# K and V loaded in tiles of two heads, 4 MB each, in a decode kernel of attention and MLP

## The chip, the core and the metric

The kernel runs on one core of a Trainium2 chip. A core has five engines with queues of their own: PE (matmul), DVE (vector), ACT (scalar functions), POOL and SP. SP here issues nearly all loads. Sixteen DMA engines move data from the chip's memory (HBM) into the core's own (SBUF, 128 partitions). The metric is device time in microseconds (us) of one execution.

## What is computed

One decode step for a batch of B = 4 rows of width D = 576. One branch is attention of 32 query heads over 16 cached key/value heads, of which the last W = 2048 keys count. The other is a small MLP. The input and both branches are summed.

```
xn = layernorm(x)
W  = min(4096, max(256, Sk // 4))                  # Sk = 8192, so W = 2048
q  = (xn @ wq) as [B, 32, 1, 128]
k, v = last W keys of k_cache, v_cache [B, 16, 8192, 128], each head used by rep = 2 query heads
o  = softmax(q k^T / sqrt(128)) v
A  = o as [B, 1, 4096] @ wo
# MLP branch with one token: the shifted parts are zero, so x1 = xn
Bm = xn + gelu(layernorm(xn) @ w3) @ w4
out = x + A + Bm
```

K and V are 33.5 MB each, the four weight matrices 20 MB together.

## The kernel before

**Tiles.** `load_kv` (L103) loads one KV head of all four batch rows as a tile of 2 MB: 32 partitions to a batch row, NC = 64 consecutive keys to a partition, 16 KB in one run. K and V tiles share a pool of six buffers (`NKV`). A DMA splits over the 16 DMA engines, eight partitions to each, so an engine moves eight packets of 16 KB for a tile.

**Loads.** All loads but x stand in SP's queue, in program order. The list `order` is K0 K1 K2 V0 K3 V1 K4 and so on, V13 V14 V15 last. `flush_loads` issues as many as there are free buffers, and the loop frees a K buffer and a V buffer at the end of each head. Ahead of V0, V4, V8 and V12 stands one of the four pieces of wo (L125, 1.18 MB, two buffers, the first of which also holds small early tiles). w3 (L130, L131) stands behind V2 and takes the buffer of wq. The rows of w4 that the tiling leaves over are x4. They lie in a K/V buffer and come in eight small pieces (L164 "A", L167 "B", L170 "C", five at L174), two behind V13, three behind V14, three behind V15 (`X_AFTER`). w4 (L153) comes last, in six pieces, and takes w3's buffer.

**One head.** DVE turns K, two quarters of a tile at a time (`k_transpose`, L256). It works on 32-bit words, each a pair of neighbouring values of the head dimension, so the even and the odd values stand alternately in `kt`, and a score matmul reads every second bf16. `k_mask` (L357) writes a large negative number into the score tile S where key rows and query rows are of different batch rows. `k_scores` adds the products, 16 matmuls of 512 columns a head (L369). Softmax: DVE takes the row maximum (L375, L377), PE brings it to eight rows (L382), DVE reduces and negates it (L387), PE subtracts it from S by a matmul over all 512 columns (L391), ACT takes the exponential with the row sum (L398), and DVE turns it into PT (L403). `pv` multiplies with V, 16 matmuls of 512 columns on four groups of 32 PE columns (L426). ACT scales the result by one over the sum (L433), PE turns it (`o_turn`, four 128x128 blocks in float32, L439), and DVE sums it (L449). For every fourth head `o_spread`, `o_pick` and `o_proj` (L458, L468, L471, L215) multiply by a piece of wo and add to an accumulator of two PSUM tiles, `accs`.

**Order.** The program writes out the order of all engines' work. In round t of the loop head t is scored, head t - 1 goes through softmax, head t - 2 through `pv`, t - 3 and t - 4 through the output. The MLP's first half (`mlp_g`, `mlp_turn`, `mlp_act`) stands in round 7. Behind the loop the last heads are finished, then come x4 and w4 (`mlp_extra`, `mlp_out`, L215), and two copies and a store end the program (L684, L686, L687).

Of the kernel before, what the change touches and what calls it, by code (L numbers as in the profile page):

```python
# [16 lines left out]
NKV = 6  # L17
BIG = 1.0e30
# [4 lines left out]
def kernel(  # L23
# [27 lines left out]
    PB = P // B  # L51
    NC = W // PB
    NJ = B * rep
    QD = 32
    NQD = P // QD
    NSL = 4
    SC = NC // NSL
    NI = 2
    CW = D // NI
    NW = SC * QD  # L60
    assert NW == 512 and NSL * NJ == QD and NQ == 2 * NQD * NW and NFH == 18
# [23 lines left out]
    ps_s = ctx.enter_context(tc.tile_pool(name="ps_s", bufs=2, space=PSUM))  # L85
# [12 lines left out]
    wo_src = A_wo.rearrange("(s p i) n -> s p (i n)", p=P, i=WOR)  # L98

    def load_kv(kind, h):  # L100
        win = k_win if kind == "K" else v_win
        t = kvp.tile([P, NC, Dh], BF16, tag="kv", name=f"{kind.lower()}n")
        nc.sync.dma_start(out=t[:].rearrange("p c d -> p (c d)"),  # L103
                          in_=win[:, h].rearrange("b (p c) d -> p b (c d)", c=NC))
        kv_tiles[kind, h] = t
# [70 lines left out]
    X_AFTER = {13: ["A", (0, 0, 3)], 14: [(1, 0, 3), "B", "C"], 15: [(2, 0, 3), (3, 0, 1), (3, 1, 3)]}  # L176

# [3 lines left out]
    ident_w = const.tile([P, P + (NSL - 1) * NJ], F32)  # L181
    ident_f = ident_w[:, 0:P]
    make_identity(nc, ident_f)
    nc.gpsimd.tensor_copy(out=ident_w[:, P:], in_=ident_w[:, 0:(NSL - 1) * NJ])
# [14 lines left out]
    ZP = (NSL - 1) * NJ  # L199
# [4 lines left out]
    accs = [ps_acc.tile([P, CW], F32, name=f"acc{i}") for i in range(2)]  # L204
    for acc in accs:
        nc.vector.memset(acc[:], 0.0)

    def acc_of(i):
        return accs[i * 2 // NI][i * QD:i * QD + B, :]
# [42 lines left out]
    def k_transpose(h, half):  # L252
        c0 = half * 2 * SC
        src = kv_tiles["K", h][:].bitcast(I32)[:, c0:c0 + 2 * SC, :].rearrange("p c (ib i) -> p ib c i", i=QD)
        kt = ktp.tile([P, 2, 2 * SC, QD], I32, tag="kt")
        nc.vector.transpose(out=kt[:], in_=src)  # L256
        kts[h, half] = kt
# [6 lines left out]
    oh4 = const.tile([P, B], F32)  # L264
    nc.vector.reduce_sum(out=oh4[:], in_=ident_f[:].rearrange("p (k b r) -> p b k r", b=B, r=rep), axis=AX.XY)
    ohk = const.tile([P, B], F32)
    nc.vector.reduce_sum(out=ohk[:], in_=ident_f[:].rearrange("p (q b) -> p b q", b=B), axis=AX.X)
    oh_ps = ps_m.tile([B, 2, P], F32, tag="m", name="oh_ps")
    nc.tensor.transpose(out=oh_ps[:, 0, :], in_=oh4[:], identity=ident_f[:])
    nc.tensor.transpose(out=oh_ps[:, 1, :], in_=ohk[:], identity=ident_f[:])  # L270
    ohT = const.tile([B, P], BF16)
    nc.scalar.activation(out=ohT[:], in_=oh_ps[:, 0, :], func=ACT.Copy)
    negbig = const.tile([B, QD], BF16)
    nc.vector.tensor_scalar(out=negbig[:], in0=oh_ps[:, 1, 0:QD], scalar1=-1.0, scalar2=BIG,
# [8 lines left out]
    with nc.allow_low_precision("zeros and ones"):  # L283
        nc.vector.reduce_sum(out=sel_g[:], in_=ident_f[:].rearrange("p (g j) -> p g j", j=NJ), axis=AX.X)
    jT_ps = ps_m.tile([NJ, P], F32, tag="m", name="jT_ps")
# [7 lines left out]

    sel_wo = const.tile([P, WOR, WOH, WOD], BF16)
    nc.scalar.activation(out=sel_wo[:], in_=ident_bf[:].rearrange("p (d i) -> p i d", i=WOR).unsqueeze(2)
                         .to_broadcast([P, WOR, WOH, WOD]), func=ACT.Copy)
    own = const.tile([P, WOH], F32)
    nc.vector.reduce_sum(out=own[:], in_=ident_f[:].rearrange("p (h d) -> p h d", h=WOH), axis=AX.X)
# [23 lines left out]
    q_sb = bigp.tile([P, 2, NQD, Dh], BF16, tag="big", name="q_sb")  # L322
# [15 lines left out]
    for kb in range(NQD):  # L338
        rows = slice(kb * QD, (kb + 1) * QD)
        dst = qz[rows, ZP:].rearrange("p (x m) -> p x m", m=P)[:, :, kb * QD:kb * QD + NJ].rearrange("p x (b r) -> p x b r", r=rep)  # L340
        src = qs_ps[rows].rearrange("p h i r b -> p (h i) b r")
        if kb % 2:
            nc.scalar.activation(out=dst, in_=src, func=ACT.Copy)
        else:
            nc.vector.tensor_copy(out=dst, in_=src)  # L345
# [9 lines left out]
    def k_mask(h):  # L355
        S_ps[h] = ps_s.tile([P, NW], F32, tag="S", name="S")
        nc.tensor.matmul(out=S_ps[h][:].rearrange("p (c k) -> p c k", k=QD), lhsT=ohT[:],  # L357
                         rhs=negbig[:].unsqueeze(1).to_broadcast([B, SC, QD]),
                         start=True, stop=False, skip_group_check=True)

    def k_scores(h, s):
        half, c0 = s // 2, s % 2 * SC
        kt = kts[h, half][:].bitcast(BF16)
        if s % 2:
            kts.pop((h, half))
        for ie in range(4):
            ib, e = divmod(ie, 2)
            z0 = (h * 4 + ie) * P + ZP - s * NJ
            nc.tensor.matmul(out=S_ps[h][:], lhsT=qz[:, z0:z0 + P],  # L369
                             rhs=kt[:, ib, c0:c0 + SC, e:2 * QD:2].rearrange("p c k -> p (c k)"),  # L370
                             start=False, stop=False, skip_group_check=True)

    def sm_max(h):
        mx = small.tile([P, 1], F32, tag="mx")
        nc.vector.reduce_max(out=mx[:], in_=S_ps[h][:], axis=AX.X)  # L375
        dm = small.tile([P, NG], BF16, tag="dm")
        nc.vector.tensor_scalar(out=dm[:], in0=sel_g[:], scalar1=mx[:, 0:1], scalar2=None, op0=ALU.mult)  # L377
        st["dm", h] = dm

    def sm_maxT(h):  # L380
# [337 lines left out]
```

## Time and profile before

| | |
|---|---|
| runs of the kernel before | median 211.43 us (211.31 to 212.11, 3 runs) |
| the profiled execution, first to last instruction | 209.5 us |
| PE busy | 150.2 us (72%) |
| DVE busy | 113.3 us (54%) |
| ACT busy | 34.9 us (17%) |
| bytes read from HBM | 87.17 MB, 416 GB/s over the span |
| score matmuls L369 | 256, 77.6 us busy |
| K turns L256 | 32, 73.5 us busy, 2298 ns each |
| PV matmuls L426 | 256, 24.3 us busy |
| exponentials L398 | 16, 9.5 us busy, 597 ns each |

The busy share of an engine is not a share of the path: DVE waits 24.0 us for K tiles to land. By stretches of the run:

| us | PE busy | DVE busy | granted PE clock | GB/s |
|---|---|---|---|---|
| 0 to 20 | 8.5 | 6.1 | 1.00 | 386 |
| 20 to 60 | 29.3 | 30.1 | 0.87 | 432 |
| 60 to 100 | 22.4 | 17.0 | 0.70 | 428 |
| 100 to 140 | 35.8 | 24.7 | 0.96 | 429 |
| 140 to 180 | 30.5 | 24.7 | 0.85 | 433 |
| 180 to 209.5 | 23.7 | 10.8 | 0.90 | 363 |

In the lines quoted further down "SPq" is SP's issue of a DMA with its duration, "PEld" the weight load of a matmul, and a bracket at the end of a line gives the engine's idle time just before it and what ended it.

### The profile page before, as it was taken

The numbers are of one execution on the slowest core, as the hardware profiler recorded it, in microseconds if no ns is written. First come the engines' busy times: TensorE is split into PE (matmuls) and PEld (weight loads), VectorE is DVE, ScalarE is ACT, GpSimd is POOL, SyncE is SP. The second block draws the span as 40 slices with busy tenths as digits, with TensorE's granted clock in tenths as the row PEclk, the third lists the DMA queues.
The fourth block names the chain that finished last, engine by engine and source line by source line (L and its number), as shares of the span: only waits on it lengthen the run. The fifth ranks groups of instructions, "written<-read, shape, count | busy, mean of one in ns | idle before, by whom it ended". The sixth has DMA issues, their size and how long they took to land.

```text
span 209.5 us, 2370 instructions
## 1 busy us (share of the span) xinstructions
PE 150.2 (72%) x972; PEld 57.8 (28%) x972; DVE 113.3 (54%) x156; ACT 34.9 (17%) x72; POOL 9.0 (4%) x32
## 2 busy tenths in 40 slices
PE   0457297698690039759998998589696856999783
PEld 0122132233130003213454332224132312343451
DVE  4511877794910083926607889276849390764110
ACT  7602201112010011110222321102111201023100
POOL 4710000000000000000001200000000000000000
PEclk9999589999797556985999999799879985699699
DMA  7999999999999999999999999999999999999992
GB/s 301 400 422 429 425 429 432 422 438 427 456 422 409 446 419 420 444 444 410 441 422 432 444 405 435 438 444 410 438 429 425 428 445 419 432 438 425 427 407 92
DMA packets 6708, 87.31 MB, mean 417 GB/s; under 512 B 761, under 2 KB 1042, under 8 KB 1706
## 3 DMA queue, kind: packets, MB, share of 16 engines
q1 hardware_dynamic: 6690, 87.17, 97.7%
q8 instruction: 7, 0.11, 0.2%
q10 hardware_dynamic: 8, 0.00, 0.0%
q14 instruction: 3, 0.02, 0.0%
HBM read 87.17 MB, written 0.00 MB: 416 GB/s over the span
## 4 chain that ended last, share of the span: by engine, by line
DMA 76%; PE 18%; DVE 3%; ACT 1%; SPq 1%; issue 1%; DVEq 0%; ACTq 0%
DMA vn<-in_A_v_cache_dram 51%; DMA kn<-in_A_k_cache_dram 12%; DMA w_sb<-in_B_w_dram 7%; DMA wq_sb<-in_A_wq_dram 6%; PE S L369 6%; PE O L426 3%; PE g_ps L499 2%; DVE kt L256 2%; PE q_ps L313 2%; PE oT L439 1%; PE acc L215 1%; PE S L391 1%; DVE qz L345 1%; PE gT_ps L521 1%; SPq L153 1%
## 5 line engine op out<-in xcount | busy, mean ns | idle before, releaser
L369 PE MATMUL S<-kt,qz 128*128 128x512 bf16 x256 | 77.6, 432 | 31.6 <-DVE kt L256 31.6
L256 DVE STREAM_TRANSPOSE kt<-kn 128x2048 int32<-128x2048 int32 x32 | 73.5, 2298 | 25.4 <-DMA kn<-in_A_k_cache_dram 24.0
L369 PEld LDWEIGHTS <-qz 128*128 128x128 bf16 x256 | 23.3, 105 | 64.7 <-issue 47.3
L426 PE MATMUL O<-vn,PT 128*32 128x512 bf16 x256 | 24.3, 424 | 9.7 <-DMA vn<-in_A_v_cache_dram 9.6
L398 ACT ACTIVATE E<-S 128x512 bf16<-128x512 f32 x16 | 9.5, 597 | 73.5 <-PE S L391 73.5
L433 ACT ACTIVATE O_sb<-O,rd 128x512 f32<-128x512 f32 x16 | 11.0, 686 | 63.8 <-DVE rd L416 48.3
L403 DVE STREAM_TRANSPOSE PT<-E 128x512 bf16<-128x512 bf16 x16 | 11.4, 710 | 14.4 <-ACT E L398 14.4
L449 DVE TENSOR_REDUCE on<-oT 128x8 bf16<-128x128 f32 x16 | 4.6, 288 | 22.0 <-PE oT L439 21.9
L426 PEld LDWEIGHTS <-PT 128*32 128x32 bf16 x256 | 5.7, 95 | 33.2 <-issue 22.1
L439 PE MATMUL oT<-ident_w,O_sb 128*128 128x128 f32 x64 | 12.7, 335 | 0.0
L375 DVE TENSOR_REDUCE mx<-S 128x1 f32<-128x512 f32 x16 | 10.5, 657 | 0.9 <-PE S L369 0.9
L439 PEld LDWEIGHTS oT<-ident_w,O_sb 128*128 128x128 f32 x64 | 8.3, 167 | 5.1 <-issue 4.7
L391 PE MATMUL S<-nm,j_row 8*128 8x512 bf16 x16 | 6.8, 428 | 1.8 <-DVE nm L387 1.7
L357 PE MATMUL S<-negbig,ohT 4*128 4x512 bf16 x16 | 6.4, 398 | 0.0
L313 PE MATMUL q_ps<-wq_sb,xnT 128*32 128x512 bf16 x40 | 4.1, 591 | 2.2 <-DMA wq_sb<-in_A_wq_dram 2.2
L215 PE MATMUL acc<-w_sb,gT 128*4 128x288 bf16 x70 | 4.9, 286 | 1.1 <-DMA w_sb<-in_B_w_dram 1.1
L499 PE MATMUL g_ps<-w_sb,ln2T 128*32 128x512 bf16 (+2 forms) x55 | 5.5, 439 | 0.0
L541 POOL TENSOR_TENSOR g_u<-g_x 128x180 f32<-128x180 f32 x1 | 0.5, 486 | 102.5 <-ACT g_x L535 102.5
L215 PE MATMUL acc<-wo_sb,op 128*4 128x288 bf16 x64 | 4.6, 286 | 0.4 <-DVE op L471 0.4
L537 DVE COPY g_x<-gT_ps 128x64 f32<-128x64 f32 x2 | 0.5, 225 | 8.1 <-PE gT_ps L521 8.1
L215 PEld LDWEIGHTS <-gT 128*4 128x4 bf16 (+3 forms) x90 | 3.8, 83 | 3.1 <-issue 1.6
L240 PE MATMUL tp<-ident_bf,first 4*128 4x4 bf16 x8 | 0.6, 172 | 5.3 <-DVE first L227 5.3
(94 smaller groups left out, 79.1 us busy)
## 6 DMA issues: line engine op xcount, KB each, us to landing
kn<-in_A_k_cache_dram SPq DMA_DIRECT2D x16, 2048.0 KB, 25.8
vn<-in_A_v_cache_dram SPq DMA_DIRECT2D x16, 2048.0 KB, 23.0
wo_sb<-in_A_wo_dram SPq DMA_DIRECT2D x4, 1152.0 KB, 38.0
w_sb<-in_B_w_dram SPq DMA_DIRECT2D x1, 4608.0 KB
wq_sb<-in_A_wq_dram SPq DMA_DIRECT2D x1, 4096.0 KB
w_sb<-in_B_w_dram SPq DMA_DIRECT2D x1, 2592.0 KB, 10.9
w_sb<-in_B_w_dram SPq DMA_DIRECT2D x2, 576.0 KB, 34.6
w_sb<-in_B_w_dram SPq DMA_DIRECT2D x1, 864.0 KB
```

Of the source, the lines that this page charges most:

```text
L215: nc.tensor.matmul(out=acc_of(i), lhsT=lhsT, rhs=rhs[:, i * CW:(i + 1) * CW], start=False, stop=False, skip_group_check=True)
L256: nc.vector.transpose(out=kt[:], in_=src)
L313: nc.tensor.matmul(out=q_ps[r][g * QD:(g + 1) * QD, :], lhsT=xnT[:, k, :], rhs=wq_sb[:, col:col + NW], start=(j == 0), stop=False, skip_gr ...
L369: nc.tensor.matmul(out=S_ps[h][:], lhsT=qz[:, z0:z0 + P], rhs=kt[:, ib, c0:c0 + SC, e:2 * QD:2].rearrange("p c k -> p (c k)"), start=False ...
L375: nc.vector.reduce_max(out=mx[:], in_=S_ps[h][:], axis=AX.X)
L391: nc.tensor.matmul(out=S_ps[h][:], lhsT=j_row[:], rhs=st.pop(("nm", h))[:, 0:1].to_broadcast([NJ, NW]), start=False, stop=False, skip_grou ...
L398: nc.scalar.activation(out=E[h][:].rearrange("p c k -> p (c k)"), in_=S_ps.pop(h)[:], func=ACT.Exp, scale=scale, accum_out=st["rs"][:, h % ...
L403: nc.vector.transpose(out=PT[h][:], in_=E.pop(h)[:])
L426: nc.tensor.matmul(out=O_ps[h][g * QD:(g + 1) * QD], lhsT=PT[h][:, c, :], rhs=vn[:, :, c, :], start=(s == 0), stop=False, skip_group_check ...
L433: nc.scalar.activation(out=O_sb[h][:], in_=O_ps.pop(h)[:], func=ACT.Copy, scale=st.pop(("rd", h)))
L439: nc.tensor.transpose(out=oT[:, s, :], in_=o[:, s, :], identity=ident_w[:, s * NJ:s * NJ + P])
L499: nc.tensor.matmul(out=out, lhsT=ln2T[:, k, :], rhs=rhs, start=(j == 0), stop=False, skip_group_check=True)
```

## The change

A K or V tile now holds two KV heads, t and t + 8, of all four batch rows: 16 partitions to a pair of batch row and head, 128 keys and 32 KB in one run to a partition, 4 MB a tile. The pool has three buffers of the doubled size, the same memory. There are eight rounds in place of 16.

A partition of K now belongs to one of two heads. Scores for both heads are taken in the same S tile: `k_scores` runs for each head e of the pair, with `qz` windows moved by four rows, and reads every fourth bf16 of `kt`, so that its 512 columns are those keys' values that a group of 16 partitions holds. There are two S tiles a pair (u = 0, 1) in a PSUM pool of three. The maximum goes back to all rows by a matmul of one column (`sm_back`), and DVE makes two biases of it (`sm_bias`), one for each head; in each the rows of the other head get a large negative number. ACT takes the exponential twice for each S tile, once with each bias, so that the other head's rows become zero. PT is then turned in 32-bit words.

`pv` has 64 matmuls of 256 columns a pair. `o_turn` turns two blocks a pair in place of eight. wo's rows are laid out for head pairs, with one piece for every second pair. The two accumulators become one PSUM tile, and `fin` takes a buffer of wo.

The loads stand as K0 K1, wo, V0, K2, V1, w3, K3, wo, V2, K4, V3, K5, wo, V4, K6, V5, K7, V6, V7, and then the eight x4 pieces, the last piece of wo and the six pieces of w4. The MLP's first half stands in round 3. The core of the diff, where lines that go are shown only if the listing above does not show them as clearly:

```diff
-NKV = 6
+NKV = 3
...
+    NPR = Hkv // rep
+    NX8 = B * rep
+    PB = P // NX8
     NC = W // PB
     QD = 32
     NQD = P // QD
+    NU = 2
+    NS2 = 2
+    SC = NC // (NU * NS2)
+    KK = QD // rep
+    NJ = B * rep * rep
...
-    wo_src = A_wo.rearrange("(s p i) n -> s p (i n)", p=P, i=WOR)
+    wo_src = A_wo.rearrange("(e s x i) n -> s x e (i n)", e=rep, s=Hkv // WOQ, i=WOR)
+    def load_kv(kind, t):
         win = k_win if kind == "K" else v_win
+        tl = kvp.tile([P, NC, Dh], BF16, tag="kv", name=f"{kind.lower()}n")
+        src = win.rearrange("b (e h) (p c) d -> h p b e (c d)", e=rep, c=NC)[t]
+        nc.sync.dma_start(out=tl[:].rearrange("p c d -> p (c d)"), in_=src.rearrange("p b e n -> p (b e) n"))
+        kv_tiles[kind, t] = tl
...
-    X_AFTER = {13: ["A", (0, 0, 3)], 14: [(1, 0, 3), "B", "C"], 15: [(2, 0, 3), (3, 0, 1), (3, 1, 3)]}
...
-    ZP = (NSL - 1) * NJ
+    ZP = (NS2 - 1) * NJ + B
...
-    accs = [ps_acc.tile([P, CW], F32, name=f"acc{i}") for i in range(2)]
+    acc = ps_acc.tile([P, CW], F32, name="acc")
...
+    def k_transpose(t, q):
+        src = kv_tiles["K", t][:].bitcast(I32)[:, q * SC:(q + 1) * SC, :].rearrange("p c (ib i) -> p ib c i", i=QD)
+        kt = ktp.tile([P, 2, SC, QD], I32, tag="kt")
         nc.vector.transpose(out=kt[:], in_=src)
+        kts[t, q] = kt
...
+    other = const.tile([P, rep], F32)
+    nc.vector.reduce_sum(out=other[:], in_=sel_j[:].rearrange("p (r e b) -> p e r b", r=rep, e=rep), axis=AX.XY)
+    nc.vector.tensor_scalar(out=other[:], in0=other[:], scalar1=-1.0, scalar2=BIG, op0=ALU.add, op1=ALU.mult)
...
+    def k_scores(t, q, e):
+        u, s = divmod(q, NS2)
+        kt = kts[t, q][:].bitcast(BF16)
+        if e == rep - 1:
+            kts.pop((t, q))
         for ie in range(4):
+            ib, odd = divmod(ie, 2)
+            z0 = ((t + NPR * e) * 4 + ie) * P + ZP - s * NJ - e * B
+            nc.tensor.matmul(out=S_ps[t, u][:], lhsT=qz[:, z0:z0 + P],
+                             rhs=kt[:, ib, :, 2 * e + odd:2 * QD:4].rearrange("p c k -> p (c k)"),
...
-    def sm_sub(h):
-        nc.tensor.matmul(out=S_ps[h][:], lhsT=j_row[:], rhs=st.pop(("nm", h))[:, 0:1].to_broadcast([NJ, NW]),
-                         start=False, stop=False, skip_group_check=True)
-
...
+    def sm_back(t):
+        bp = ps_m.tile([P, 1], F32, tag="m", name="bp")
+        nc.tensor.matmul(out=bp[:], lhsT=j_row[:], rhs=st.pop(("nm", t))[:], start=True, stop=True)
+        st["bp", t] = bp
+
+    def sm_bias(t):
+        bias = small.tile([P, rep], F32, tag="bias")
+        nc.vector.tensor_scalar(out=bias[:], in0=other[:], scalar1=st.pop(("bp", t))[:, 0:1], scalar2=scale,
+                                op0=ALU.add, op1=ALU.mult)
+        st["bias", t] = bias
+
+    def sm_exp(t, u):
+        if u == 0:
+            st["rs", t] = small.tile([P, NU, rep], F32, tag="rs", name="rs")
+        E[t, u] = ptp.tile([P, SC // 2, QD, 2], BF16, tag="e", name="E")
+        src = S_ps.pop((t, u))[:].rearrange("p (c o k) -> p c o k", o=2, k=KK)
+        for e in range(rep):
+            nc.scalar.activation(out=E[t, u][:, :, e:QD:rep, :].rearrange("p c k o -> p c o k"), in_=src,
+                                 func=ACT.Exp, scale=scale, bias=st["bias", t][:, e:e + 1],
+                                 accum_out=st["rs", t][:, u, e:e + 1])
+
+    def sm_turn(t, u):
+        PT[t, u] = ptp.tile([P, SC // 2, QD], I32, tag="pt", name="PT")
+        nc.vector.transpose(out=PT[t, u][:], in_=E.pop((t, u))[:].rearrange("p c k o -> p c (k o)").bitcast(I32))
+
...
+    def pv(t, u, lo, hi):
+        if u == 0 and lo == 0:
+            O_ps[t] = ps_o.tile([P, NS2, Dh], F32, tag="O", name="O")
+        vn = kv_tiles["V", t][:].rearrange("p (u s c) d -> p u s c d", u=NU, s=NS2)
+        pt = PT[t, u][:].bitcast(BF16)
+        for c in range(lo, hi):
+            g = c % NQD
+            nc.tensor.matmul(out=O_ps[t][g * QD:(g + 1) * QD], lhsT=pt[:, c // 2, c % 2:2 * QD:2], rhs=vn[:, u, :, c, :],
+                             start=(u == 0 and c < NQD), stop=False, skip_group_check=True)
+        if hi == SC:
+            PT.pop((t, u))
+
...
+    order = [("K", 0), ("K", 1)]
+    for t in range(NPR):
+        order.append(("V", t))
+        if t + 2 < NPR:
+            order.append(("K", t + 2))
+    order.append(("X", 0))
...
     def flush_loads():
         while pos["n"] < len(order) and pos["free"] > 0:
-            kind, h = order[pos["n"]]
-            if kind == "V" and h % WOQ == 0:
-                load_wo(h // WOQ)
+            kind, t = order[pos["n"]]
             if kind == "X":
                 load_x4()
+                for p in ("A", (0, 0, 3), (1, 0, 3), "B", "C", (2, 0, 3), (3, 0, 1), (3, 1, 3)):
+                    x4_rows(p)
+                load_wo(Hkv // WOQ - 1)
+                load_w4()
             else:
-                load_kv(kind, h)
-            if kind == "X" or kind == "V" and h > min(X_AFTER):
-                for part in X_AFTER.get(h, []):
-                    x4_rows(part)
+                if kind == "V" and whole(t + 1) and t + 2 < NPR:
+                    load_wo(t * rep // WOQ)
+                load_kv(kind, t)
+            if (kind, t) == ("V", 1):
+                load_w3()
             pos["n"] += 1
             pos["free"] -= 1
-            if (kind, h) == W3_AFTER:
-                load_w3()
-        if pos["n"] == len(order):
-            pos["n"] += 1
-            load_w4()
+    def free_one():
+        pos["free"] += 1
+        flush_loads()
...
+    for t in range(NPR):
+        a, o = t - 1, t - 2
+        if a >= 0:
+            sm_max(a, 1)
+        if o >= 0:
+            o_scale(o)
+        k_transpose(t, 1)
+        if t == G_AT:
+            mlp_g(0)
+        k_mask(t, 0)
+        k_scores(t, 0, 0)
+        if a >= 0:
+            sm_maxT(a)
+            sm_neg(a)
+        k_scores(t, 0, 1)
+        if a >= 0:
+            sm_back(a)
+            sm_bias(a)
+            sm_exp(a, 0)
+            sm_exp(a, 1)
+        k_transpose(t, 2)
+        if t == G_AT:
+            mlp_g(1)
+            mlp_turn(0)
+        k_scores(t, 1, 0)
+        if o >= 0:
+            o_turn(o)
+        k_scores(t, 1, 1)
+        if a >= 0:
+            sm_turn(a, 0)
+        if o >= 0:
+            o_sum(o)
+        k_transpose(t, 3)
+        free_one()
+        if a >= 0:
+            sm_turn(a, 1)
+        if t == G_AT:
+            mlp_g(2)
+            mlp_turn(1)
+        k_mask(t, 1)
+        k_scores(t, 2, 0)
+        if a >= 0:
+            sm_den(a)
+            sm_rec(a)
+            pv(a, 0, 0, SC // 2)
+        k_scores(t, 2, 1)
+        sm_max(t, 0)
+        if o >= 0:
+            o_spread(o)
+        if a >= 0:
+            pv(a, 0, SC // 2, SC)
+        if o >= 0:
+            o_pick(o)
+        if t == G_AT:
+            mlp_turn(2)
+            mlp_act()
+        if t + 1 < NPR:
+            k_transpose(t + 1, 0)
+        k_scores(t, 3, 0)
+        if a >= 0:
+            pv(a, 1, 0, SC // 2)
+        k_scores(t, 3, 1)
+        if a >= 0:
+            pv(a, 1, SC // 2, SC)
+            free_one()
+        if o >= 0:
+            o_proj(o)
+    hl = NPR - 1
+    sm_max(hl, 1)
+    o_scale(hl - 1)
     sm_maxT(hl)
     sm_neg(hl)
+    o_turn(hl - 1)
+    sm_back(hl)
+    sm_bias(hl)
+    sm_exp(hl, 0)
+    sm_exp(hl, 1)
+    o_sum(hl - 1)
+    sm_turn(hl, 0)
+    sm_turn(hl, 1)
     sm_den(hl)
     sm_rec(hl)
+    pv(hl, 0, 0, SC)
+    pv(hl, 1, 0, SC)
     o_scale(hl)
+    mlp_extra(XB, XS)
...
-    fin = const.tile([B, D], out.dtype)
+    fin = wop.tile([B, D], out.dtype, tag="wo", name="fin")
```

## The prediction

> **What bounds the kernel now.** I read the page first: the row of DMA slices, the queue table and the chain.
>
> ```profile
> span 209.5 us, 2370 instructions
> ...
> DMA  7999999999999999999999999999999999999992
> ...
> q1 hardware_dynamic: 6690, 87.17, 97.7%
> ...
> DMA 76%; PE 18%; DVE 3%; ACT 1%; SPq 1%; issue 1%; DVEq 0%; ACTq 0%
> ```
>
> The slices stand at 9 from the second to the second last. The load queue's packets take 97.7% of 16 engines' span, and the last-ended chain is 76% DMA. No engine comes near that (PE 72%, DVE 54%), so the time is what 16 DMA engines need for 87.17 MB, plus a head and a tail.
>
> What one packet costs I counted from the trace's packet records. Of the 4,096 packets of 16,384 bytes (all of K and V) nearly all took 611 ns. The 9,216-byte ones of wo took 347, those of 20,736 (w4) 771, 127 of the 128 packets of 36,864 (w3) 1,364, and half of the 128 of 32,768 (wq) 1,213. All lie on one line: 8 ns, plus the bytes at 27.2 GB/s an engine. Every load ends with one more packet of 9 ns on each engine. Between first load and last the slowest engine is never without a packet.
>
> Second, the issue side: SP's part of the timeline (start, duration, line), where L125 loads wo, L164 to L174 load the eight pieces of x4, and L153 loads w4.
>
> ```profile
> 0.74 0.39 SPq L120 DMA_DIRECT2D wq_sb<-in_A_wq_dram  x1
> ...
> 145.06 0.46 SPq L125 DMA_DIRECT2D wo_sb<-in_A_wo_dram  x1
> ...
> 170.03 0.25 SPq L167 DMA_DIRECT2D x<-in_B_w_dram  x1
> 174.89 0.84 SPq L170 DMA_DIRECT2D x<-in_B_w_dram  x1
> 179.77 0.57 SPq L103 DMA_DIRECT2D vn<-in_A_v_cache_dram  x1
> 184.77 0.82 SPq L174 DMA_DIRECT2D x<-in_B_w_dram  x3
> 189.62 5.72 SPq L153 DMA_DIRECT2D w_sb<-in_B_w_dram  x6
> ```
>
> And SP's waits (line, what it waited for, us in total, times, longest):
>
> ```profile
> SPq L153 <- DMA vn<-in_A_v_cache_dram: 6.8, 2, 4.0
> ...
> SPq L170 <- DMA vn<-in_A_v_cache_dram: 4.6, 1, 4.6
> SPq L174 <- DMA vn<-in_A_v_cache_dram: 4.4, 1, 4.4
> SPq L167 <- DMA wo_sb<-in_A_wo_dram: 2.3, 1, 2.3
> ```
>
> The last row is the one to learn from. L167 loads an x4 piece into a tile that wo does not touch, yet its issue waits 2.3 us for wo to land. In issue order that wo stands exactly eight loads ahead. L170, next in order, waits for the V tile eight ahead of it, and w4's first piece waits for V14, again eight ahead. So a load is issued only when the load eight issues earlier has landed; the built program says the same (eight semaphores, taken in turn). Today this is free: at 189.62, when w4 is first issued, all of V15 (4.9 us) still stands in the rings.
>
> Third, the tail of the timeline:
>
> ```profile
> 194.66 1.59 PE L426 MATMUL O<-vn,PT 128*32 128x512 bf16 x16 [0.99 <-DMA vn<-in_A_v_cache_dram]
> ...
> 204.44 0.78 PE L215 MATMUL acc<-w_sb,gT 128*4 128x288 bf16 x10 [0.44 <-DMA w_sb<-in_B_w_dram]
> ...
> 205.85 1.02 PE L215 MATMUL acc<-w_sb,gT 128*4 128x288 bf16 x12 [0.63 <-DMA w_sb<-in_B_w_dram]
> ...
> 206.90 0.45 DVE L684 CAST fin<-acc 4x288 bf16<-4x288 f32 x1 [7.04 <-PE acc L215]
> ```
>
> V15 landed at 194.52 on its slowest engine, and the PV matmuls began at once. The last w4 piece landed at 206.53, and the PE had only twelve matmuls left. The end follows the last w4 packet by 3.0 us.
>
> **The change, part by part.**
>
> *Packets.* K and V go from 256 packets of 16 KB on each engine to 128 of 32 KB. 256 x 611 ns = 156.42 us, 128 x 1,213 = 155.26: -1.15. Sixteen fewer loads, each with one closing packet of 9 ns per engine: -0.14. Together -1.3. Bounds: wq's mean was 1,231 ns, since its packets ran in the first 6 us with the start's irregularities; at that, 128 x 1,231 = 157.6, +1.2 instead of -1.15. I take 1,213, as w3's longer packets later lie on the same line.
>
> [...]
>
> *Buffers: 3 x 4 MB for 6 x 2 MB.* Does the queue run dry in the middle? Count from the moment a K tile lands. DVE frees it after four transposes of 2.30 us (L256), one maximum and its product (0.65 + 0.23), nm 0.12, a bias of about 0.2 (as dm's row), PT 0.7 and on 0.3: 11.4 us, about 12 with the waits on PE. The load that wants this buffer is V of the same pair. Ahead of it in the rings stand V of the pair before and the next K, 2 x 8 x 1.213 = 19.4 us, so its issue may come that late at no cost. Cover: 7 us. V's buffer comes free some 7.5 us after V landed (half the scores, all PV, one projection, by the tail's rows of 1.07 and 0.40 to 0.83), and has 12 us of cover. PE has 32 score matmuls a pair at 77.6/256 = 0.303, so 9.7, PV 24.3/8 = 3.0, masks 0.8, turns 0.7, small ones 1.2: 15.4 us of 19.4. The MLP pair adds some 6 us but has the 2.8 us of a wo load beside it, and eats cover only. So the middle costs nothing. Without cover every microsecond over 19.4 a pair counts seven times.
>
> *Softmax, PV and the output turn.* The subtracting matmul (L391, 6.8 us), 48 of 64 output turns (9.5 of 12.7) and half the scales go. A one-column matmul, a bias and twice the exps come (32 x (0.60 + 0.20) = 25 us of ACT, now 13). PV has the same columns in 512 matmuls. All of it lies under the loads. Scores now read every fourth bf16 of kt, where they read every second; no row of before shows such a read as moving data. Bounds: nothing, or the whole 0.265 us again (four took 1.06). I take nothing: the reads at every second element run as fast as PV's contiguous ones. [...]
>
> *Order at the end.* This is the part on the path. After V7 SP issues eight x4 pieces, then wo's last piece, then w4. The eighth x4 piece stands eight issues behind V7. By the rule of the waits it is issued when V7 has landed, and wo and w4 stand behind it on SP. All that is left in the rings then is seven small x4 pieces on a few engines, so the rings run empty. Before, from V15's landing to w4's took 206.53 - 194.52 = 12.01; with wo's 8 x 0.347 = 2.8 that would be 14.8 without a gap. With it: 0.03 for SP to wake, 0.25 for the x4 issue, then from wo's issue to its landing beyond the mere stream. The nearest row is the start of the run, where the rings were empty too: wq's small piece was issued at 0.74 and landed at 4.05, and its stream is 8 x 0.159 = 1.27, so 2.03 us. Then the stream, 2.8 + 8 x 0.771 + 8 x (0.262 + 0.220 + 0.178) + 16 x 0.051 + closing packets = 15.1. Sum 17.4, so the gap costs 2.6. Low bound: the output store had its first packet 0.76 after its issue and a landing lag of 0.35, 1.11 in place of 2.03: 1.7. High: 3.0, with another issue of 0.4 in the way. The x4 pieces no longer delay V on the slowest engine: V13 landed 5.04 after K15 where eight packets need 4.90, so -0.15.
>
> *PE after the last loads.* V7 should land near 190.3 and w4's first piece near 201.5. PE by then needs softmax, PV, turn and projection of pair 7: pair 7's scores end near 188, and the chain by its rows (maximum 0.9, three small steps 1, four exps 3.2, PT 0.7, den and rd 0.7, PV 2.6, scale 0.6, turn to pick 2.3, projection 1.15) is 13 us, near 201. The cover is that w4's first 36 matmuls (2.4 us) fit in the 4 us until its next pieces; without it up to 1 us. The two accumulators now share a bank; if that makes the two fin copies follow each other, +0.4.
>
> **Sum.** -1.3 - 0.15 + 2.6 = +1.15 on 209.53: 210.7. The runs lie around 211.43, 1.9 above the profiled execution; I carry the difference over: 212.6.
>
> **Rivals.** *No gap (faster).* If the eighth x4 issue passes without V7, w4 follows on and only -1.45 is left: 210.0. For it: the same queue never ran dry before. Against it: four rows of waits. Chance 0.13.
>
> *Dearer packets.* If two heads' packets cost what wq's did on average, +1.2 in place of -1.15: 214.9. For it: wq is the only row with 32 KB; against it: w3. 0.09.
>
> *PE becomes the bound.* If each score matmul costs another 0.265, PE needs 15.4 + 8.5 = 23.9 us a pair, over the loads' 19.4: 23.6 (first K landed) + 8 x 23.9 + 13 = 228, about 230 by the runs. It decides once a score matmul takes (19.4 - 15.4)/32 = 0.13 more. For it: no row of such a stride; against: stride two is free. 0.06.
>
> **Numbers.** The forecast has 0.72. Half a per cent (1.06 us) is about what a measurement can tell. The forecast's own range is 211.7 (low gap) to 213.4 (high gap, fin in series), and its middle lies just above the line: 0.40 slower, 0.30 same, 0.02 faster. With the rivals: slower 0.55, same 0.30, faster 0.15. The range 210.2 to 214.8 leaves out half of the first two rivals and all of the third, 0.17.
>
> **What would show it.** In SP's timeline the last L178 issue comes within 0.1 us of V7's landing, with wo at once behind it; in the slices one DMA digit falls about 15 us before the last landing; K and V packets take 1,213 ns; DVE and PE wait for K and V landings in every pair, not the loads for them. I am wrong if SP issues wo before V7 lands, if DMA shows a hole elsewhere, or if the scores' mean grows.

## The result, and the profile after

| | kernel before | changed kernel |
|---|---|---|
| median of the runs, us | 211.37 (211.15 to 212.11) | 386.29 (382.43 to 388.69) |
| profiled execution: span, us | 209.5 | 383.5 |
| GB/s over the span | 417 | 228 |

The changed kernel takes 1.82 times as long (ratio 1.8203, 95% interval 1.8104 to 1.8301), where 212.6 us had been forecast. (One of its four runs, 388.69 us, lay over 1.5% above the fastest and is left out of the ratio.) First the row of GB/s of the kernel before, then the page of the changed kernel's profile, with the rows that answer to those of before:

```profile
GB/s 301 400 422 429 425 429 432 422 438 427 456 422 409 446 419 420 444 444 410 441 422 432 444 405 435 438 444 410 438 429 425 428 445 419 432 438 425 427 407 92
```

```profile
span 383.5 us, 2748 instructions
...
DMA  8999999999999999999999999999999999999394
GB/s 346 311 219 212 210 246 219 208 208 208 208 207 362 326 212 226 211 200 212 221 219 208 208 215 222 224 212 208 214 212 219 205 208 215 217 212 212 89 428 187
...
q1 hardware_dynamic: 4386, 87.17, 97.1%
...
DMA 37%; another core or an unknown queue 35%; PE 17%; DVE 8%; issue 1%; SPq 1%; ACT 0%; DVEq 0%
```

The DMA row alone would show nothing: its slices stand at 9 as before, and the queue's packets still take 97% of 16 engines' span. Busy here means that packets are under way. What they move is in the GB/s row: 200 to 246 GB/s in most slices, where the kernel before has 400 to 456 but for its first and last. The exceptions are the slices with wq at the start (346, 311), with w3 (362, 326) and with w4 (428). So the engines are as busy as ever, and K and V arrive at half the rate. (The chain could not place 35% of the span; nothing below rests on it.)

In the packet records, the 32,768-byte packets of K and V took 2,508 ns in the median, those of wq, with the same size and in the same run, 1,213. Summed over all packets and divided by 16 engines that makes 317.9 us for K and V, against 156.7 before: 161.2 of the 174.0 us by which the span grew. The packets of wo beside them took 4.9 us more, those of w3 1.1; most of what is left is time in which some engines had no packet.

Who waits, in the waits of DVE and of SP in the changed kernel (engine, line, what it waited for, us in total, times, longest):

```profile
DVE kt L256 <- DMA kn<-in_A_k_cache_dram: 170.4, 8, 39.3
```

```profile
SPq L108 <- DMA kn<-in_A_k_cache_dram: 101.3, 7, 29.6
...
SPq L178 <- DMA vn<-in_A_v_cache_dram: 22.4, 2, 18.8
```

DVE has nothing to turn until K lands: 170.4 us, for 24.0 before. SP's issues of K and V (L108) wait for earlier loads to land, too, and for another 144.8 us for buffers that DVE and PE free; the latter costs nothing, since the engines have packets all the while. In SP's own timeline (start, us, issue) stands the end of the queue:

```profile
337.86 23.33 SPq L178 DMA_DIRECT2D x<-in_B_w_dram  x3
361.23 0.60 SPq L129 DMA_DIRECT2D wo_sb<-in_A_wo_dram  x1
361.89 3.26 SPq L157 DMA_DIRECT2D w_sb<-in_B_w_dram  x6
```

V7, the last V tile, landed at 360.95. The last of the three issues in the first row came at 360.97 and wo's at 361.23, as the prediction had it, and the slice around them holds the low DMA digit (3, with 89 GB/s; the last slice's 4 is the end). But that costs a few microseconds of 174. The tail of the timeline:

```profile
360.99 3.60 PE L437 MATMUL O<-vn,PT 128*32 128x256 bf16 x64 [2.69 <-DMA vn<-in_A_v_cache_dram]
...
379.43 1.01 PE L216 MATMUL acc<-w_sb,gT 128*4 128x288 bf16 x12 [0.67 <-DMA w_sb<-in_B_w_dram]
...
380.49 0.45 DVE L702 CAST fin<-acc 4x288 bf16<-4x288 f32 x1 [11.12 <-PE acc L216]
380.97 0.40 ACT L704 ACTIVATE fin<-acc 4x288 bf16<-4x288 f32 x1 [15.85 <-DVE fin L702]
```

PV starts with V7's landing, the last twelve matmuls follow w4's last pieces, the two fin copies come one after the other, and the kernel ends 3.4 us after the last landing (380.12).

### The profile page after: what moved, and what is told of

Same layout as the page of the kernel before. It is cut to its first block, busy times and chain, and to the rows that moved or that the text cites. A ratio compares the mean times of both kernels' runs of the same rounds, so it can differ in the third digit from the quotient of the medians.

```text
span 383.5 us, 2748 instructions
## 1 busy us (share of the span) xinstructions
PE 183.2 (48%) x1148; PEld 65.5 (17%) x1163; DVE 113.4 (30%) x156; ACT 55.9 (15%) x99; POOL 9.0 (2%) x32
## 4 chain that ended last, share of the span: by engine, by line
DMA 37%; another core or an unknown queue 35%; PE 17%; DVE 8%; issue 1%; SPq 1%; ACT 0%; DVEq 0%
DMA kn<-in_A_k_cache_dram 21%; PE S L371 13%; DMA vn<-in_A_v_cache_dram 12%; DVE kt L256 6%; DMA w_sb<-in_B_w_dram 4%; PE O L437 1%; PE g_ps L511 1%; DVE mx L377 0%; PE gT_ps L533 0%; SPq L157 0%; ACT E L410 0%; DVE PT L416 0%; PE acc L216 0%; PE oT L450 0%
## 5 line engine op out<-in xcount | busy, mean ns | idle before, releaser
L371 PE MATMUL S<-kt,qz 128*128 128x512 bf16 x241 | 119.5, 626 | 108.6 <-DVE kt L256 104.3
L256 DVE STREAM_TRANSPOSE kt<-kn 128x2048 int32<-128x2048 int32 x32 | 73.7, 2307 | 175.5 <-DMA kn<-in_A_k_cache_dram 170.4
L410 ACT ACTIVATE E<-S,bias 128x512 bf16<-128x512 f32 x32 | 39.8, 1411 | 150.3 <-DVE bias L400 150.3
L437 PE MATMUL O<-vn,PT 128*32 128x256 bf16 x512 | 26.5, 349 | 62.2 <-DMA vn<-in_A_v_cache_dram 62.2
L371 PEld LDWEIGHTS <-qz 128*128 128x128 bf16 x256 | 25.3, 113 | 161.2 <-issue 158.1
L437 PEld LDWEIGHTS <-PT 128*32 128x32 bf16 x512 | 14.6, 115 | 79.9 <-issue 78.0
L444 ACT ACTIVATE O_sb<-O,rd 128x256 f32<-128x256 f32 x8 | 3.8, 474 | 119.7 <-PE O L437 119.7
L416 DVE STREAM_TRANSPOSE PT<-E 128x512 int32<-128x512 int32 x16 | 11.1, 693 | 7.5 <-ACT E L410 7.5
L410 ACT ACTIVATION_READ_ACCUMULATOR E<-S,bias 128x1 f32 x32 | 9.1, 283 | 0.0
L420 PE MATMUL dn<-rs,same_j 128*128 128x4 f32 x16 | 2.7, 238 | 5.3 <-ACT E L410 5.3
L420 PEld LDWEIGHTS dn<-rs,same_j 128*128 128x128 f32 x16 | 3.4, 219 | 9.5 <-ACT E L410 7.5
L460 DVE TENSOR_REDUCE on<-oT 128x16 bf16<-128x128 f32 x8 | 2.1, 266 | 9.7 <-PE oT L450 9.7
```

The lines of the kernel that those rows point to most:

```text
L371: nc.tensor.matmul(out=S_ps[t, u][:], lhsT=qz[:, z0:z0 + P], rhs=kt[:, ib, :, 2 * e + odd:2 * QD:4].rearrange("p c k -> p (c k)"), start=F ...
L410: nc.scalar.activation(out=E[t, u][:, :, e:QD:rep, :].rearrange("p c k o -> p c o k"), in_=src, func=ACT.Exp, scale=scale, bias=st["bias", ...
L416: nc.vector.transpose(out=PT[t, u][:], in_=E.pop((t, u))[:].rearrange("p c k o -> p c (k o)").bitcast(I32))
L420: nc.tensor.matmul(out=dn[:], lhsT=same_j[:], rhs=st.pop(("rs", t))[:].rearrange("p u e -> p (u e)"), start=True, stop=True)
L437: nc.tensor.matmul(out=O_ps[t][g * QD:(g + 1) * QD], lhsT=pt[:, c // 2, c % 2:2 * QD:2], rhs=vn[:, u, :, c, :], start=(u == 0 and c < NQD) ...
L444: nc.scalar.activation(out=O_sb[t][:], in_=O_ps.pop(t)[:], func=ACT.Copy, scale=st.pop(("rd", t))[:, 0:1])
```

## The experiments

Three parts of the change could be at work: how K and V are loaded, how its tiles are read and written on the chip, and the order at the end. They are taken in that order.

### The load by itself

**loads_alone** has loads only, in stages of three tiles of 4 MB (2 MB in the last stage), each stage with a packet size of its own by which its records can be told apart. The forms, as partition groups x partitions within a group (comments added, dots where lines are left out):

```diff
+    def whole(i, r, n):    # [128]
...
+        src = flat[i * P * N:(i + 1) * P * N].rearrange("(p n) -> p n", n=N)
+    def heads(i, r, n):    # [16, 8], as in the change
...
+        src = win.rearrange("b (e h) (p c) d -> h p b e (c d)", e=2, c=128)[i].rearrange("p b e n -> p (b e) n")
+    def near(i, r, n):     # [16, 8], the eight 512 KB apart
...
+        src = flat[i * P * N:(i + 1) * P * N].rearrange("(x p n) -> p x n", x=8, n=N)
+    def far4(i, r, n):     # [32, 4], the four 16 MB apart
...
+        src = A_k_cache[0:2, :, 0:4096, :].rearrange("b (e h) (p c) d -> h p b e (c d)", e=2, c=128)[i]
...
+        dst = t[k:P:8, 0:n] if apart else t[16 * k:16 * k + 16, 0:n]
```

> A kernel of loads alone: no computing, the output is zeros. Stages of three loads of 4 MB (the packet sizes, each 256 bytes smaller than the last, tell the stages apart): 1 all 128 partitions from one contiguous stretch (32,768 bytes); 2 the changed kernel's K pattern, 16 key groups x 8 pairs of batch row and head 16 MB apart (32,512); 3 the same 16 x 8 form, but the eight only 512 KB apart in HBM (32,256); 4 32 key groups x 4, 16 MB apart (32,000); 5 64 x 2, 16 MB apart (31,744); 6 contiguous source, eight loads of 16 rows into every eighth partition (31,488); 7 the same source into 16 neighbouring partitions (31,232); 8 stage 2 with packets of 16 KB (16,384). [...] Theory H (HBM addresses many MB apart at a power of two collide): stages 2, 4 and 5 slow, stage 8 too, stages 1, 3, 6 and 7 at 1.2. Theory S (32 KB packets of two heads are slow by themselves): 2, 4 and 5 slow, 8 fast at 0.61.

| stage | packet, bytes | median, ns |
|---|---|---|
| [128], contiguous | 32,768 | 1,213 |
| [16, 8], 16 MB apart (the change's form) | 32,512 | 2,524 |
| [16, 8], 512 KB apart | 32,256 | 2,505 |
| [32, 4], 16 MB apart | 32,000 | 1,189 |
| [64, 2], 16 MB apart | 31,744 | 1,180 |
| 16 rows into every eighth partition | 31,488 | 2,440 |
| 16 rows into 16 neighbouring partitions | 31,232 | 4,107 |
| [16, 8] with half the bytes | 16,384 | 1,264 |

The stages also stand one after another in the page's slices:

```profile
DMA  8999999999999999999999999999999899998996
GB/s 328 460 427 263 210 210 210 210 210 208 208 208 208 208 208 362 423 449 417 423 448 203 203 207 210 203 197 132 117 110 142 107 136 110 114 139 123 212 215 139
```

From 427 to 460 GB/s the rate falls to 210 for both forms of 16 x 8, rises to 417 to 449 for 32 x 4 and 64 x 2, falls to 203 to 210, then to 107 to 142 (122 by the mean packet), and ends at 212 to 215. Distance in HBM does not decide: 16 MB apart is fast with 32 x 4, and 512 KB apart is slow with 16 x 8. Nor does the packet's size: 16 KB packets double too (1,264 ns, for 611 in the kernel before). The two stages of 16 rows load the same rows of HBM in the same order and differ only in the partitions that they fill: 2,440 ns against 4,107. So which partitions are filled at one time counts. 16 rows at a time into 16 neighbouring partitions are the slowest of the eight forms.

**near_16x8** puts that to the whole kernel: the change's form, with pieces near each other in HBM.

```diff
-        win = k_win if kind == "K" else v_win
+        win = A_k_cache if kind == "K" else A_v_cache
...
-        src = win.rearrange("b (e h) (p c) d -> h p b e (c d)", e=rep, c=NC)[t]
-        nc.sync.dma_start(out=tl[:].rearrange("p c d -> p (c d)"), in_=src.rearrange("p b e n -> p (b e) n"))
+        src = win[t // 2, t % 2 * 8:t % 2 * 8 + 2].rearrange("h (x p c) d -> p (h x) (c d)", x=4, c=NC)
+        nc.sync.dma_start(out=tl[:].rearrange("p c d -> p (c d)"), in_=src)
```

> The changed kernel with its 16 x 8 form of loads, but read from 4 MB that lie together (the eight pieces 512 KB apart; other keys, so the output is not the reference's). [...] Theory H: packets near 1,213 ns, about 212 us.

387.0 us in one run, K and V packets at 2,507 ns: as slow as the change.

**split_32x4** keeps the change and its 32 KB packets, and takes the partitions as 32 groups of 4. That needs other keys: two batch rows and twice the window.

```diff
-        win = k_win if kind == "K" else v_win
+        win = (A_k_cache if kind == "K" else A_v_cache)[0:2, :, 0:2 * W, :]
```

> The changed kernel, but each K or V load reads 32 key groups x 4 pairs (two batch rows, two heads, still 16 MB apart, packets still 32 KB): 4,096 keys of half the batch, so the values are other keys' and the output is not the reference's. Same bytes, same work on all engines. [...] Theory H: packets stay near 2,490 ns, about 386 us.

218.85 us (ratio to the kernel before 1.0355, 1.0314 to 1.0395), over the 212.6 of the forecast, which had counted packets at 1,213 ns. The packets are back at 1,213 ns, V7 lands at 191.0, and of the 174.9 us between the medians 167.4 are gone.

**before_16x8** is the reverse: this one thing put into the kernel before.

```diff
-        win = k_win if kind == "K" else v_win
+        win = A_k_cache if kind == "K" else A_v_cache
...
-                          in_=win[:, h].rearrange("b (p c) d -> p b (c d)", c=NC))
+                          in_=win[h % B, h].rearrange("(y p c) d -> p y (c d)", y=8, c=NC))
```

> The kernel before with one thing of the change put in: each 2 MB load of K or V (16 KB a packet as before) takes its partitions as 16 rows of 8 instead of all 128 in one, here from the keys of one batch row. It reads other keys, so the output is not the reference's. [...] Theory of the tile's size or of the layout of heads and keys: packets stay at 611 ns and the kernel at 210 to 213 us.

376.35 us in one run. Its page:

```profile
span 374.5 us, 2356 instructions
...
GB/s 336 308 219 212 268 207 215 212 216 219 382 316 213 212 258 219 208 219 217 217 212 219 219 243 221 219 222 215 212 219 222 209 253 218 210 221 225 256 385 51
...
L369 PE MATMUL S<-kt,qz 128*128 128x512 bf16 x242 | 101.6, 557 | 95.2 <-DVE kt L256 92.3
```

The same half rate, without a tile of two heads, a 32 KB run or a new read. The 16,384-byte packets went from 611 to 1,244 ns in the median. Their sum per engine grew by 154.5 us, nearly by the 156.7 that it had been. The time grew by 165, and wo's packets, which run beside them, make 4.8 of the rest. The L369 row is of use below.

So K and V lost their rate by the 16 x 8 form alone. Why this form is slow was not shown. The two stages of 16 rows in loads_alone tell that it matters where a load is written, but which engine fills which partitions no record here names. And the form of a load changes the order in which HBM is read as well; no run kept that order with a destination at full rate, so how much of the factor of two is the writing stays open.

### How the tiles are read and written

split_32x4 is still 7.6 us slower than the kernel before, and its loads are not what ends it. First two rows of the kernel before (busy time in us, mean ns of one, idle before), then split_32x4:

```profile
L369 PE MATMUL S<-kt,qz 128*128 128x512 bf16 x256 | 77.6, 432 | 31.6 <-DVE kt L256 31.6
...
L398 ACT ACTIVATE E<-S 128x512 bf16<-128x512 f32 x16 | 9.5, 597 | 73.5 <-PE S L391 73.5
```

```profile
PE   0446299999999970299999999999999999972884
...
DMA  7999999999999899999999999999999999949950
...
PE 59%; DMA 32%; DVE 4%; ACT 2%; issue 0%; SPq 0%; DVEq 0%; ACTq 0%
...
L371 PE MATMUL S<-kt,qz 128*128 128x512 bf16 x256 | 124.7, 626 | 17.6 <-DVE kt L256 17.6
...
L410 ACT ACTIVATE E<-S,bias 128x512 bf16<-128x512 f32 x32 | 39.7, 1406 | 63.0 <-DVE bias L400 63.0
```

TensorE (the engine PE) is full for most of the span, and the chain is 59% PE, where before it was 76% DMA. One score matmul takes 626 ns in the mean, before 432, and one exp 1,406, before 597. Four matmuls in a row take 1.97 us, before 1.07.

**scores_4_bytes** takes away the read of every fourth value, and **exp_contiguous** the write of exp, the exponential on ScalarE (the engine ACT), to every second pair of values; **both_steps_mended** has both edits.

```diff
# scores_4_bytes, both_steps_mended
-                             rhs=kt[:, ib, :, 2 * e + odd:2 * QD:4].rearrange("p c k -> p (c k)"),
+                             rhs=kt[:, ib, e * SC // 2:(e + 1) * SC // 2, odd:2 * QD:2].rearrange("p c k -> p (c k)"),
# exp_contiguous, both_steps_mended
-            nc.scalar.activation(out=E[t, u][:, :, e:QD:rep, :].rearrange("p c k o -> p c o k"), in_=src,
+            nc.scalar.activation(out=E[t, u][:, e * SC // 4:(e + 1) * SC // 4].rearrange("p c k o -> p c (k o)")
+                                 .rearrange("p c (y o k) -> p (c y) o k", o=2, k=KK), in_=src,
```

> split_32x4 with the score matmul's moving read at a step of two bf16 values instead of four (half of the keys' rows, both heads of each; output not the reference's). Theory of the step: four score matmuls go from 1.97 us back to 1.07 to 1.2, TensorE's 178 us fall by 40 or more, TensorE stops setting the end, and the time is that of the loads, whose last one ended at 210.2 us in split_32x4, and some 3.5 us behind it: 212.5 to 214.5 us. Theory of the clock (the matmuls were long because the granted clock was 0.93): they stay at 1.8 us or more and the time within 1 us of 218.9.

> split_32x4 with exp writing its result in one run instead of every second pair of values (the output is not the reference's). Theory of the written step: exp falls from 1.40 to 0.60 us and ScalarE's 40 us by more than 20; TensorE still sets the end, so only the four exps behind the last scores count, and the time falls by 1.5 to 3.5 us, to 215.4 to 217.4. If exp's length comes from its reads or from its count of 32, it stays at 1.3 us or more and the time at 218 to 220.

> split_32x4 with both of the last two edits (output not the reference's): what the change would be with tiles of two heads and 32 KB runs, without its partition split and without its strided reads and writes. The loads' end of split_32x4, 210.2 us, and 3.5 us behind it: 212.5 to 214.5 us, which would be what the prediction said of the order at the end. If there is another cost in the larger tiles, over 215.

The groups of scores_4_bytes and of exp_contiguous (busy time in us, mean ns of one, idle before):

```profile
L371 PE MATMUL S<-kt,qz 128*128 128x512 bf16 x241 | 78.0, 448 | 41.0 <-DVE kt L256 38.7
...
L410 ACT ACTIVATE E<-S,bias 128x512 bf16<-128x512 f32 x32 | 39.6, 1399 | 75.7 <-DVE bias L400 75.7
```

```profile
L371 PE MATMUL S<-kt,qz 128*128 128x512 bf16 x241 | 119.5, 626 | 22.2 <-DVE kt L256 17.8
...
L410 ACT ACTIVATE E<-S,bias 128x512 bf16<-128x512 f32 x32 | 21.6, 686 | 64.0 <-DVE bias L400 63.3
```

Each edit mends its own row and leaves the other: 448 ns for a score matmul, 686 for an exp. scores_4_bytes took 215.54 us (1.0192, 1.015 to 1.0234), 3.3 below split_32x4, and its chain is 67% DMA again. The clock is not the cause. The granted clock is 1.00 or 0.50 at any one time in these traces, and in stretches of one clock a score matmul took, in the mean:

| run, stretch in us | granted clock | read | ns |
|---|---|---|---|
| split_32x4, 94.5 to 175 | 1.00 | every fourth | 626 |
| split_32x4, 84.2 to 94 | 0.50 | every fourth | 626 |
| kernel before, 100 to 133 | 1.00 | every second | 388 |
| kernel before, 66 to 82 | 0.50 | every second | 620 |

So in these stretches the wide step costs 238 ns a matmul at a granted clock of 1.00, and 6 at 0.50. The means of 432 and 448 above mix the two clocks.

exp_contiguous took 217.75 us (1.0284, 1.0228 to 1.034). It is 1.1 below split_32x4 where 1.5 or more was expected, and the two intervals overlap: with TensorE as the bound its worth stays open. Without that bound it is worth nothing: both_steps_mended took 215.57 us (1.0195, 1.0156 to 1.0235), the same as scores_4_bytes. Both lie above their expected 212.5 to 214.5.

### The order at the end

**split_32x4_three_x4** stands on split_32x4, the strided read still in it. It loads x4 in three pieces, so that none stands eight issues behind V7.

```diff
-                for p in ("A", (0, 0, 3), (1, 0, 3), "B", "C", (2, 0, 3), (3, 0, 1), (3, 1, 3)):
-                    x4_rows(p)
+                x4_rows("A")
+                x4_rows("B")
+                x4_rows("C")
...
-            src = B_w4[X0:X0 + 16, :].rearrange("(q i) n -> q i n", q=4)[:, 3]
-            nc.sync.dma_start(out=t[0:4, (XB + 3) * D:XC * D], in_=src)
+            src = B_w4[X0:X0 + 16, :].rearrange("(q i) n -> q (i n)", q=4)
+            nc.sync.dma_start(out=t[0:4, XB * D:XC * D], in_=src)
```

> split_32x4 with x4 loaded in three pieces instead of eight, so that the eighth issue behind V7 is a piece of w4 with wo and most of w4 already in the rings. [...]

It took 220.65 us (1.0418, 1.0356 to 1.048), no better than split_32x4, where the forecast had counted 2.6 us for the gap. The loads ended 3.2 us sooner (207.0 for 210.2), and the kernel did not. Its last matmuls wait on TensorE's own work, and ran at a lower granted clock: 0.50 from 200 to 208 us, for 0.71 in split_32x4. A gap in the loads costs nothing here, where the loads do not set the end. (The 206.2 of the next expectation is the landing of the fourth of w4's six pieces in this run; the last landed at 206.98.)

**both_mended_three_x4** is the same edit on both_steps_mended, where loads set the end again.

> both_steps_mended with x4 in three pieces (output not the reference's), so that no x4 issue stands eight behind the last V and the wo and w4 issues go out before it lands. Theory of the dry queue: in both_steps_mended the end of the loads, 210.1 us, holds some 4 us in which the queue ran dry; without them w4's last packet lands near 206.2 as in split_32x4_three_x4, and the kernel takes 211.3 to 212.2 us, the time of the kernel before. Theory of TensorE's chain behind the last V tile (ready at 202.5 us in both_steps_mended, then 70 matmuls of 0.07 to 0.09 us and 3.1 us of copies and store): it ends at 210.5 to 211.8, so 212.4 to 213.7 us, and half of the 4 us is lost to it. Theory that the gap costs nothing: within 0.5 us of 215.6.

212.47 us (1.0059, 1.0042 to 1.0076), 3.1 less than both_steps_mended. That lies in the range of the second theory, but not by its chain: TensorE was ready for w4 at 201.0, and the end followed w4's last landing by 3.6 us, for 3.5 in both_steps_mended. Here are the windows around V7's landing, first of both_steps_mended (eight pieces), then of both_mended_three_x4; the last columns are granted clock, DMA share and GB/s:

```profile
186.00:189.00 3.00, 3.00 (x44) 1.68 (x40) 1.09 (x3) 0.48 (x1) 0.00 (x0) 1.00 0.94 405
189.00:193.00 4.00, 0.80 (x19) 0.73 (x22) 1.90 (x5) 2.79 (x8) 0.00 (x0) 1.00 0.35 83
193.00:197.00 4.00, 4.00 (x70) 2.53 (x64) 0.16 (x1) 0.47 (x1) 0.00 (x0) 0.53 1.02 409
```

```profile
186.00:189.00 3.00, 3.00 (x44) 1.70 (x40) 1.08 (x3) 0.47 (x1) 0.00 (x0) 1.00 0.93 397
189.00:193.00 4.00, 0.80 (x19) 0.69 (x23) 1.86 (x5) 2.78 (x8) 0.00 (x0) 1.00 1.00 422
193.00:197.00 4.00, 4.00 (x76) 2.62 (x66) 0.20 (x2) 0.47 (x1) 0.00 (x0) 0.57 1.00 429
```

With eight pieces the DMA engines are 65% idle for 4 us. From V7's landing to w4's last one it is 19.42 us (190.68 to 210.10), with three pieces 15.98 (190.87 to 206.85): the gap costs the loads 3.4 us at their end, and the kernel 3.1. Up to w4's third piece (207.62 and 203.78) the difference is 4.0. The run with three pieces loses some of it at the fourth, during which a 16 KB packet of the queue q8 ("instruction" in the page) ran for 0.97 us; that this packet is the reason is not tested.

**before_order_alone** puts that order into the kernel before, with nothing else of the change.

```diff
-        if h == min(X_AFTER):
-            order.append(("X", h))
+    order.append(("X", 0))
...
-            if kind == "V" and h % WOQ == 0:
+            if kind == "V" and h % WOQ == 0 and h < Hkv - WOQ:
...
+            if kind == "X":
+                for part in ("A", (0, 0, 3), (1, 0, 3), "B", "C", (2, 0, 3), (3, 0, 1), (3, 1, 3)):
+                    x4_rows(part)
+                load_wo(Hkv // WOQ - 1)
```

> The kernel before with only the change's order at the end: the eight x4 pieces behind the last V, then wo's last piece, then w4; K and V of one head, 16 KB packets, all 128 partitions in one as before. Theory of the dry queue: V15 lands 2.8 us sooner, near 191.7, the eighth x4 piece is issued with that landing, and from there to w4's last packet it takes 19.4 us as in both_steps_mended, so the loads end near 211.1 and the kernel takes 215.5 to 217 us. By the 2.6 us of the prediction: 213 to 214.5. If the order is free: 211.0 to 211.8.

215.20 us (1.0178, 1.0149 to 1.0208), just under the expected range and above that of the prediction. SP's timeline:

```profile
181.93 9.89 SPq L174 DMA_DIRECT2D x<-in_B_w_dram  x3
191.86 0.36 SPq L125 DMA_DIRECT2D wo_sb<-in_A_wo_dram  x1
192.26 3.27 SPq L153 DMA_DIRECT2D w_sb<-in_B_w_dram  x6
```

V15 landed at 191.58; wo was issued 0.28 us after it, and w4's last packet landed at 210.31, 18.7 us after V15. The kernel before needs 12.0 and 2.8 for wo: the gap is 3.9 us, and the kernel's time grew by 4.0.

Put together, from run to run:

| from | to | us |
|---|---|---|
| changed kernel 386.29 | split_32x4 218.85 | 167.4, the partitions |
| split_32x4 218.85 | scores_4_bytes 215.54 | 3.3, the strided read |
| scores_4_bytes 215.54 | both_steps_mended 215.57 | 0.0, the strided write |
| both_steps_mended 215.57 | both_mended_three_x4 212.47 | 3.1, the gap |
| both_mended_three_x4 212.47 | kernel before 211.24 | 1.2, the rest |

In the rest, by the two profiled executions, are w4's last landing (206.85 for 206.53) and a longer end behind it (3.6 us for 3.0), in which the two fin copies still follow each other (0.5 us). No run beats the kernel before, and a load of the change's own keys that avoids 16 x 8 was not tried.

## Why the prediction was wrong, by its steps

**The packets' price: the step that failed.** The sum took K and V at 1,213 ns a packet, 155.26 us, and they took 317.9. The price was wq's, and the line that it lay on with w3's was taken as leave for the whole load. But both of those load all 128 partitions in one run, and the new load differs from them and from the K and V of before: 16 groups of 8 partitions instead of 32 groups of 4. That its pieces lie 16 MB apart in HBM is not it: 512 KB apart they took 2,507 ns (near_16x8). The rival "dearer packets" priced 1,231 ns for a packet that took 2,508, because both of its bounds came from loads with all 128 partitions in one run, wq and w3. No row of before showed a load in 16 groups, and its upper bound was missing.

**Packets.** In every run of two-head tiles without the 16 x 8 form 1,213 ns held, and K and V took 155.4 to 155.6 us an engine for 156.7. V7 landed at 190.7 to 191.0, where 190.3 was said: against V15 in before_order_alone (191.58) 0.6 to 0.9 of the -1.3 arrived. It is right nearly to its size, for a load that the change does not make. The -0.15 for x4 came too: V15 landed 2.94 sooner there, 2.8 of it wo.

**Buffers.** Right as far as it could be seen: in both mended runs no slice in the middle shows a DMA digit under 9. One sign did not hold: the loads do wait for buffers, 144.8 us in the changed kernel and 108.2 in both_steps_mended. It cost nothing there, as the prediction's cover has it: the DMA digits stay at 9.

**Softmax and scores: "I take nothing".** Wrong, and hidden by the larger loss. The score matmuls take 124.7 us in split_32x4 for 77.6 before, 0.18 each more, between the bounds of 0 and 0.265. That is over the 0.13 from which the third rival was to decide, and it did decide there: TensorE became the bound, at 218.85 rather than the rival's 230, since the read cost less than the whole 0.265. The free read was carried over from a step of two values (432 ns for a score matmul, 424 for PV's contiguous one, by the page of before) to a step of four, and is not borne out there: four matmuls took 1.97 us at 8 bytes a step, 1.07 at 4, and only at a granted clock of 0.50 was the difference small (626 ns for 620 each). The exp's price was off too, 1.40 us for 0.60, because a write of every second pair was priced by a row with a contiguous one; ScalarE had room for it.

**Order at the end.** The mechanism was right to the issue: the eighth piece went out 0.02 us after V7's landing, wo and w4 behind it, and the queue ran dry. The size was low: 3.4 to 4.0 us for 2.6, over the upper bound of 3.0. The terms that were too small: in both_steps_mended wo landed 5.99 us after its issue, where 2.03 and 2.8 had been counted, with packets of 445 ns in the mean for 347 (0.8 us over an engine's eight), and w4 landed 13.15 us behind wo, where 12.3 were left of the sum. In before_order_alone wo took 5.02 and w4 13.44. Why the loads take longer behind the gap is open.

**The rest.** The fin copies in series (+0.4) were right: 0.48 us apart in the tail above. Pair 7 ready near 201 was right too, where loads do not hold it up: w4's matmuls start at 201.0 in both_mended_three_x4. Had the partitions and the read been as assumed, the time would be that of both_steps_mended, 215.57, and the forecast of 212.6 still 3 us low and its range exceeded: by the profile, 2.0 from V7's landing to w4's last (19.42 for 17.4), 0.4 by V7's landing (190.68 for 190.3) and 0.5 behind the last landing, with the fin copies in series.

## What to carry to other kernels

When a load's shape changes, look beyond packet size and address at how its outermost dimension cuts the partitions: here 32 groups of 4 moved some 420 GB/s and 16 groups of 8 moved 210, with the DMA row at 9 in both, so read the GB/s row beside it. A row prices only loads of its own form; what differs still needs a bound, or a few loads run alone. And a tile's read for TensorE should keep the step of what was measured: twice the step cost 0.18 us a matmul in the mean, and made TensorE the bound once the loads were fast again.

## What the runs showed of the hardware

- DMA into the on-chip memory at 31 to 32 KB a packet: 1,180 to 1,213 ns with the partitions in one run of 128, in 32 x 4 or in 64 x 2, 2,440 to 2,524 with 16 groups of 8 or every eighth partition, 4,107 into 16 neighbouring partitions (loads_alone). The engines count as busy throughout: DMA digits of 9 at 200 to 246 GB/s (changed kernel) as at 400 to 456 (kernel before).
- A matmul of 512 columns that reads every fourth bf16 took 626 ns at a granted clock of 1.00 and of 0.50 alike (split_32x4), with every second 388 at 1.00 and 620 at 0.50 (kernel before): the time at the wide step did not follow the clock.
- An exp of 512 columns that writes 4 bytes out of every 8 took 1,406 ns (split_32x4), with one contiguous run 597 (kernel before) to 686 (exp_contiguous).
- The queue that had run dry cost more than its idle time: 2.7 us without a packet in the mean of the engines, 3.4 us at the last landing (both_steps_mended), and the first load behind the gap had packets of 445 ns in the mean for 347.
- On this queue loads waited for the one eight issues earlier to land: in the kernel before an x4 piece (L167) waited 2.3 us for wo, which fills another tile. In the changed kernel and in both_steps_mended the eighth issue behind V7 came 0.02 us after its landing.
